# Attention inside a three-part kernel: masks by matmul, value rows in the host's layout, means spread by Pool

## The chip, the cores and the metric

One core of a Trainium2 chip runs one program. The metric is the device time of one execution in microseconds (us); of a kernel the median of its runs is taken.

## The reference

Three parts follow one another. The first is an attention in which each query sees the 31 keys around it and 24 block maxima of the keys; the second a mixture of experts in which each token goes to its best expert; the third a second mixture with a fixed capacity for each expert. The change touches the first alone:

```python
B, H, S, D = q.shape                      # 4, 8, 768, 64
block, window = (32, 16)
k_sum = k.reshape(B, H, nb, block, D).max(axis=3)
v_sum = v.reshape(B, H, nb, block, D).mean(axis=3)
scores_l = scale * np.matmul(q, k.transpose(0, 1, 3, 2))
mask_l = np.abs(pos[:, None] - pos[None, :]) < window
scores_s = scale * np.einsum('bhsd,bhnd->bhsn', q, k_sum) + np.log(block)
scores_l_m = np.where(mask_l, scores_l, -1000000000.0)
scores_all = np.concatenate([scores_l_m, scores_s], axis=-1)
a = np.exp(scores_all - np.max(scores_all, axis=-1, keepdims=True))
a = a / (np.sum(a, axis=-1, keepdims=True) + 1e-09)
return np.matmul(a, np.concatenate([v, v_sum], axis=2))
```

## The kernel before, in words

The attention (function `phase_a`) works on eight units, each a batch element and four of its eight heads. A unit is six steps, so there are 48 steps; a step takes two head pairs by two windows of 64 queries, that is four score tiles of 128 rows (64 queries of each of two heads) by 118 columns: 24 block maxima and 94 keys around the window. Masked columns and the logarithm of the block size come from a table in `cst`, which also holds an identity matrix.

One loop over `i` issues the work of several steps at once, and each engine runs its own part in that order:

- `qk(i)`, L124: four query-key matmuls into a PSUM tile `s_ps` (two buffers). Then VectorE, for each of the four, adds the mask, multiplies by -0.125, writes the result to `s_sb` in SBUF and keeps the minimum in `nm` (one custom instruction and one that reads its accumulator, L132).
- `ptr(i-2)`, L140: four transposes of the weights into `pt_ps` (two buffers), copied to SBUF by ScalarE (L145).
- `ex(i-1)`, L134: four exponentials on ScalarE from `s_sb`, with `nm` as bias (L138). In the loop `ptr` stands ahead of `ex`.
- `pv(i-3)`, L147: sixteen half-width matmuls with the value rows `VV` (three buffers), whose last column of ones gives the sum; VectorE divides (L156 to L164) into `X`.
- In the second unit of each batch element, `post` and `logits` (L165 to L181): transposes of the finished rows, and the router's logits. The routing of the first mixture follows in a few stages on VectorE and Pool, tied to later steps (`gate1` to `gate3`, `first1` to `first3`).
- For the next unit: block maxima (`prep_k`, VectorE), a second set of keys (`prep_k2`, VectorE), the maxima copied into both key tiles (`prep_kc`, L108 and L109, VectorE), the queries spread into a block-diagonal tile (`prep_q`, L112, half by ScalarE and half by VectorE).

`load(u)` issues a unit's transfers on SP's queue, in program order: keys and queries of two head pairs, then the means of the unit before, then values `v` for the means, then the value rows. `prep_v` (L113) makes the means of a unit: Pool adds 32 rows pairwise in SBUF (L118), scales (L120), and four DMAs on SP's queue spread the 24 means of each head to the twelve windows of `VV`:

```python
for h in range(4):
    nc.sync.dma_start(vv[0:24,:,h,0:64],vs2[24*h:24*h+24,None,:].to_broadcast([24,12,64]))
```

What sets the order around the change is thus program order alone, by the loop's lags (`LAGS=(1,2,3)`) and the tables `SHIFT`, `EARLYK` and `STAGES`. A DMA in SP's queue that waits holds up all that stands behind it, and so does a waiting instruction on VectorE, ScalarE or Pool.

Behind the loop come the rest of the routing, the first mixture (`phase_b`) and the second (`phase_d`), which run matmuls with weights split into a high and a low part by ScalarE, VectorE and Pool (L504, L505).

Of the kernel before, what the change touches and what calls it, by code (L numbers as in the profile page):

```python
# [7 lines left out]
AF=mybir.ActivationFunctionType; OP=mybir.AluOpType; AX=mybir.AxisListType  # L8
# [15 lines left out]
def layout(inp):  # L24
    q,k,v=inp['q'],inp['k'],inp['v']
    qd=np.ascontiguousarray(q.reshape(B,4,2,S,D).transpose(0,2,4,1,3)).reshape(B,128,4,S)
    kd=np.zeros((B,2,D,4,KW),np.float32)
# [8 lines left out]

    j=np.arange(94)[None,:]; c=np.arange(128)[:,None]%64
    band=(j>=c)&(j<=c+30)
    m=np.zeros((3,128,118),np.float32)
    m[:,:,:24]=np.float32(8*np.log(32))  # L40
    ok=[band&(j>=15), band, band&(j<=78)]
    for i in range(3): m[i,:,24:]=np.where(ok[i],0.0,NEG)
    cst=np.concatenate([m.transpose(1,0,2).reshape(128,354),np.eye(128,dtype=np.float32)],1).astype(np.float32)
    return dict(q=qd,k=kd,v65=vd,v=np.ascontiguousarray(v),w17=w17,cst=np.ascontiguousarray(cst))

def phase_a(nc,tc,ctx,I,st):
# [27 lines left out]
    def load(u):  # L74
        b,g=units[u]
        kt=ld.tile([128,2,KW],F32,name="kt",bufs=3); qd=ld.tile([128,2,S],F32,name="qd"); vn=st["raw"].tile([128,2048],F32,name="wraw")[0:96]
        vv=VV[u%3]; src=I['v65']
        def ld_k(h0,h1): nc.sync.dma_start(kt[:,h0:h1],I['k'][b,:,2*g+h0:2*g+h1,:])
        def ld_q(h0,h1): nc.sync.dma_start(qd[:,h0:h1],I['q'][b,:,2*g+h0:2*g+h1,:])
        def ld_v():  # L80
            nc.sync.dma_start(vn,I['v'][b,4*g:4*g+4].rearrange("h (n k) d -> (h n) (k d)",k=32))
        def ld_vv():
            for (s0,s1) in ((0,6),(6,12)):
                ap=bass.AP(tensor=src.tensor,offset=src.offset+(b*2+g)*VR*260+64*260*s0,ap=[[260,VP],[64*260,s1-s0],[1,260]])
                nc.sync.dma_start(vv[24:24+VP,s0:s1].rearrange("p s h d -> p s (h d)"),ap)
# [23 lines left out]
        cpy(d['k2'][:,h,:,0:24],ks)  # L109
    def prep_q(u,h,half,cpy):  # L110
        d=U[u]; qd,q2=d['qd'],d['q2']; r=64*half
        cpy(q2[r:r+64,h,:,r:r+64],qd[r:r+64,h].rearrange("p (t c)->p t c",c=64))  # L112
    def prep_v(u,eng):  # L113
        d=U[u]; vn,vv=d['vn'],d['vv']
        vs2=wk.tile([96,64],F32,name="vs2",bufs=2); w=1024
        if eng is V: V.tensor_reduce(vs2,vn[:,w:2*w].rearrange("p (k d)->p d k",d=64),AX.X,OP.add); w//=2
        while w>=64:
            G.tensor_tensor(vn[:,0:w],vn[:,0:w],vn[:,w:2*w],op=OP.add); w//=2  # L118
        if eng is V: G.tensor_tensor(vn[:,0:64],vn[:,0:64],vs2,op=OP.add)
        G.tensor_scalar(vs2,vn[:,0:64],1.0/32,None,op0=OP.mult)  # L120
        for h in range(4):
            nc.sync.dma_start(vv[0:24,:,h,0:64],vs2[24*h:24*h+24,None,:].to_broadcast([24,12,64]))
    X={}; XT={}; D={}
    def qk(i):  # L124
        u,pairs=steps[i]; d=U[u]
        p=ps.tile([128,4,128],F32,name="s_ps")
        for j,(h,w) in enumerate(pairs):
            T.matmul(p[:,j,0:118],d['q2'][:,h,w,:],d['k2'][:,h,w//2,:] if w%2 else d['kt'][:,h,64*w:64*w+118],start=True,stop=True)  # L128
        sb=wk.tile([128,4,118],F32,name="s_sb"); nm=wk.tile([128,4],F32,name="nm")
        for j,(h,w) in enumerate(pairs):  # L130
            mk=mask[:,0 if w==0 else (2 if w==11 else 1),:]
            V.tensor_tensor_reduce(out=sb[:,j,:],in0=p[:,j,0:118],in1=mk,scale=-0.125,scalar=3e38,op0=OP.add,op1=OP.min,accum_out=nm[:,j:j+1])  # L132
        D['sb',i]=(sb,nm)
    def ex(i):  # L134
        sb,nm=D.pop(('sb',i))
        pe=wk.tile([128,4,118],F32,name="p_e")
        for j in range(4):
            A.activation(pe[:,j,:],sb[:,j,:],AF.Exp,bias=nm[:,j:j+1],scale=-1.0)  # L138
        D['pe',i]=pe
    def ptr(i):  # L140
        pt=ps.tile([118,4,128],F32,name="pt_ps")
        pe=D.pop(('pe',i))
        for j in range(4): T.transpose(pt[:,j,:],pe[:,j,:],ident)
        pts=wk.tile([118,4,128],F32,name="pt_sb",bufs=5)
        A.copy(pts,pt)  # L145
        D['pt',i]=pts
# [981 lines left out]
```

## Time and profile before

| what | us |
|---|---|
| median of 3 runs (687.06 to 688.77) | 687.66 |
| the profiled execution | 682.42 |
| its span, first to last instruction | 680.8 |
| PE (TensorE matmuls) busy | 604.4 |
| DVE (VectorE) busy | 508.0 |
| POOL busy | 359.0 |
| ACT (ScalarE) busy | 314.2 |

Busy times are of the whole span and of stages with different limits: the loop of the attention is its first quarter. PE counts matmuls, whose ends are modelled; weight loads stand apart as PEld. The share of the DMA engines can pass 1, since packets overlap. A wait is put down to what came last.

### The profile page before, as it was taken

To read this page: it belongs to the slowest core of one execution; us is meant where nothing else is said; L and a number is where in the kernel's file an instruction comes from. 1 tells how busy PE (TensorE), PEld (TensorE's weight loads), DVE (VectorE), ACT (ScalarE), POOL (GpSimd) and SP (SyncE) were. 2 spreads that over 40 slices of the span, in tenths; PEclk is the share of its full clock that TensorE was granted. 3 is DMA by queue.
4 is the path that set the end of the run, shared out by engine and by line. 5 is a ranking of instruction groups with operands and counts; after the bars stand their busy time and mean duration, and the time that the engine had idled before them with its cause. 6 is when DMAs were issued, how large, how long until landed. Compare 5 with 4: busy or idle time off the path is not lost.

```text
span 680.8 us, 12765 instructions
## 1 busy us (share of the span) xinstructions
PE 604.4 (89%) x4424; PEld 494.0 (73%) x4427; DVE 508.0 (75%) x1896; ACT 314.2 (46%) x672; POOL 359.0 (53%) x388
## 2 busy tenths in 40 slices
PE   8769896899788999989447999999999999999996
PEld 5658775778466776666226778888797978879895
DVE  5788985999896899994675778788888888862120
ACT  6557774787235676461014235162533426154521
POOL 5234323535462463761016359494876939399841
PEclk9889997999689999898559999999999999999999
DMA  9999999969309968610026063453626254385201
GB/s 258 256 241 249 241 234 206 281 115 339 136 16 324 294 207 287 204 62 23 2 87 208 2 227 115 166 175 124 202 76 203 79 187 155 139 258 180 105 1 46
DMA packets 59778, 114.22 MB, mean 168 GB/s; under 512 B 13537, under 2 KB 23521, under 8 KB 58944
## 3 DMA queue, kind: packets, MB, share of 16 engines
q1 hardware_dynamic: 49968, 79.37, 40.6%
q0 software_dynamic: 9744, 34.02, 15.1%
q8 instruction: 35, 0.57, 0.4%
q14 instruction: 31, 0.25, 0.1%
HBM read 96.54 MB, written 14.88 MB: 164 GB/s over the span
## 4 chain that ended last, share of the span: by engine, by line
PE 18%; issue 11%; POOL 11%; DVE 6%; DMA 3%; ACT 1%; POOLq 1%; DVEq 0%
POOL wl L932 9%; PE dh_ps L961 3%; PE dh_ps L962 3%; PE dh_ps L963 3%; DMA xg<-xrows,p_ix 2%; PE dz_ps L975 2%; PE dz_ps L976 2%; PE dz_ps L977 2%; POOL out_dram L982 2%; DMA wraw<-in_w1b_dram 1%; DVE p_g L793 1%; PE rt_ps L806 1%; PE dx_ps L895 1%; PE dh_ps L950 1%; ACT wh L923 1%
## 5 line engine op out<-in xcount | busy, mean ns | idle before, releaser
L932 POOL TENSOR_TENSOR wl<-wraw,wh 128x512 fp32r<-128x512 f32 x124 | 155.4, 1297 | 5.9 <-ACT wh L923 5.5
L961 PE MATMUL dh_ps<-dxh,wh 128*128 128x384 f32 x256 | 89.2, 349 | 0.7 <-ACT dxh L953 0.7
L923 ACT CAST wh<-wraw 128x512 fp32r<-128x512 f32 x128 | 73.7, 620 | 33.8 <-DMA wraw<-in_w1b_dram 33.4
L962 PE MATMUL dh_ps<-dxl,wh 128*128 128x384 f32 x256 | 86.3, 337 | 0.5 <-DVE dxl L953 0.5
L963 PE MATMUL dh_ps<-dxh,wl 128*128 128x384 f32 x256 | 86.1, 336 | 0.0
L118 POOL TENSOR_TENSOR wraw<-wraw 96x512 f32<-96x512 f32 (+4 forms) x39 | 39.9, 1023 | 80.2 <-DMA wraw<-in_v_dram 77.8
L975 PE MATMUL dz_ps<-wh,dhh 128*128 128x512 f32 x192 | 79.0, 411 | 0.0
L977 PE MATMUL dz_ps<-wh,dhl 128*128 128x512 f32 x192 | 76.0, 396 | 0.0
L976 PE MATMUL dz_ps<-wl,dhh 128*128 128x512 f32 x192 | 75.9, 395 | 0.0
L968 DVE SCALAR_TENSOR_TENSOR dhl<-dh_ps,dhh 128x384 fp32r<-128x384 f32 x64 | 35.1, 554 | 49.0 <-ACT dhh L966 48.7
L982 POOL DMA_INDIRECT out_dram<-dz,io x24 | 24.5, 1023 | 79.5 <-ACT dz L980 76.8
L966 ACT ACTIVATE dhh<-dh_ps 128x384 fp32r<-128x384 f32 x64 | 31.5, 492 | 75.7 <-PE dh_ps L963 74.8
L505 POOL TENSOR_TENSOR wl<-wraw,wh 128x512 fp32r<-128x512 f32 (+1 forms) x26 | 47.8, 1861 | 26.2 <-ACT wh L504 22.7
L980 ACT COPY dz<-dz_ps 128x512 f32<-128x512 f32 x24 | 14.1, 587 | 102.8 <-PE dz_ps L977 56.8
L138 ACT ACTIVATE p_e<-s_sb,nm 128x118 f32<-128x118 f32 x192 | 59.7, 385 | 1.1 <-DVE nm L132 1.1
L128 PE MATMUL s_ps<-kt,Q 128*128 128x118 f32 x192 | 41.4, 299 | 11.6 <-DVE kt L108 9.1
L939 POOL DMA_INDIRECT xg<-xrows,p_ix x24 | 23.3, 972 | 50.9 <-DVE rrow L871 31.3
L961 PEld LDWEIGHTS dh_ps<-dxh,wh 128*128 128x128 f32 x256 | 48.4, 189 | 1.5 <-ACT dxh L953 0.9
L962 PEld LDWEIGHTS dh_ps<-dxl,wh 128*128 128x128 f32 x256 | 48.2, 188 | 1.3 <-DVE dxl L953 1.1
L963 PEld LDWEIGHTS dh_ps<-dxh,wl 128*128 128x128 f32 x256 | 48.1, 188 | 0.0
L504 ACT CAST wh<-wraw 128x1024 fp32r<-128x1024 f32 (+1 forms) x48 | 44.2, 983 | 7.3 <-DMA wraw<-in_w1a_dram 7.1
L132 DVE CUSTOM_DVE_ANT_0 s_sb<-s_ps,cst 128x118 f32<-128x118 f32 x192 | 42.0, 275 | 5.3 <-PE s_ps L128 3.5
(359 smaller groups left out, 1466.5 us busy)
## 6 DMA issues: line engine op xcount, KB each, us to landing
wraw<-in_w1b_dram SPq DMA_DIRECT2D x15, 1024.0 KB
wraw<-in_w2b_dram POOLq DMA_DIRECT2D x14, 1024.0 KB, 7.5
wraw<-in_w2a_dram SPq DMA_DIRECT2D x12, 1024.0 KB
wraw<-in_w1a_dram SPq DMA_DIRECT2D x10, 1024.0 KB
VV<-in_v_dram SPq DMA_DIRECT2D x16, 585.0 KB
kt<-in_k_dram SPq DMA_DIRECT2D x16, 412.0 KB
qd<-in_q_dram SPq DMA_DIRECT2D x16, 384.0 KB
wraw<-in_v_dram SPq DMA_DIRECT2D x8, 768.0 KB
```

The source lines that it names most:

```text
L132: V.tensor_tensor_reduce(out=sb[:,j,:],in0=p[:,j,0:118],in1=mk,scale=-0.125,scalar=3e38,op0=OP.add,op1=OP.min,accum_out=nm[:,j:j+1])
L138: A.activation(pe[:,j,:],sb[:,j,:],AF.Exp,bias=nm[:,j:j+1],scale=-1.0)
L504: (hi.tensor_copy if hi else nc.scalar.copy)(h[:,c],t[:,c])
L505: (lo or nc.vector).tensor_tensor(l[:,c],t[:,c],h[:,c].bitcast(F32),op=OP.subtract)
L923: A.copy(h[:,c],t[:,c])
L932: eng.tensor_tensor(l[:,c],t[:,c],h[:,c].bitcast(F32),op=OP.subtract)
L961: T.matmul(q,wh[:,c],s['xh'][:,d,:],start=(d==0),stop=False)
L962: T.matmul(q,wh[:,c],s['xl'][:,d,:],start=False,stop=False)
L963: T.matmul(q,wl[:,c],s['xh'][:,d,:],start=False,stop=(d==3))
L975: T.matmul(q,s['hh'][:,f,c0],wh[:,c],start=(f==0),stop=False)
L976: T.matmul(q,s['hh'][:,f,c0],wl[:,c],start=False,stop=False)
L977: T.matmul(q,s['hl'][:,f,c0],wh[:,c],start=False,stop=(f==7))
```

## The change

The mask is no longer added by VectorE. For each step TensorE first multiplies the identity by two mask tables at a time into `s_ps`, as the start of the sum, and the query-key matmuls add to it. The factor -0.125 moves into `prep_q`, the mask's sign and size change on the host, VectorE takes one minimum over all four tiles, and the exponentials read `s_ps` in PSUM. `s_ps` has three buffers and `pt_ps` one; `ex` stands ahead of `ptr`. The host lays value rows out so that three windows of a partition lie in one piece, and the values for the means are loaded by two DMAs. The means go by four small DMAs to one tile of 24 partitions, and Pool copies them into the twelve windows.

```diff
@@ layout
-NEG=-8e9
+NEG=-1e9
+    vd=vd.reshape(B,2,VR,260)[:,:,np.arange(VP)[:,None]+64*np.arange(12)[None,:]].reshape(B,2,VP,4,780)
+    vd=np.concatenate([vd,np.zeros((B,2,VP,4,4),np.float32)],4)
-    m[:,:,:24]=np.float32(8*np.log(32))
+    m[:,:,:24]=-np.float32(np.log(32))
-    for i in range(3): m[i,:,24:]=np.where(ok[i],0.0,NEG)
+    for i in range(3): m[i,:,24:]=np.where(ok[i],0.0,-NEG)
@@ phase_a
+    def sps(): return ps.tile([128,4,128],F32,name="s_ps",bufs=3)
@@ load
-            nc.sync.dma_start(vn,I['v'][b,4*g:4*g+4].rearrange("h (n k) d -> (h n) (k d)",k=32))
+            vs=I['v'][b,4*g:4*g+4].rearrange("h (n k) d -> (h n) (k d)",k=32)
+            for c in (0,1024): nc.sync.dma_start(vn[:,c:c+1024],vs[:,c:c+1024])
-            for (s0,s1) in ((0,6),(6,12)):
-                ap=bass.AP(tensor=src.tensor,offset=src.offset+(b*2+g)*VR*260+64*260*s0,ap=[[260,VP],[64*260,s1-s0],[1,260]])
-                nc.sync.dma_start(vv[24:24+VP,s0:s1].rearrange("p s h d -> p s (h d)"),ap)
+            for s0 in (0,2): nc.sync.dma_start(vv[24:24+VP,3*s0:3*s0+6].rearrange("p (a s) h d -> p a (s h d)",s=3),src[b,g,:,s0:s0+2,0:780])
@@ prep_q
-        cpy(q2[r:r+64,h,:,r:r+64],qd[r:r+64,h].rearrange("p (t c)->p t c",c=64))
+        o,i=q2[r:r+64,h,:,r:r+64],qd[r:r+64,h].rearrange("p (t c)->p t c",c=64)
+        if cpy is A.copy: A.mul(o,i,-0.125)
+        else: V.tensor_scalar(o,i,-0.125,None,op0=OP.mult)
@@ prep_v
-        for h in range(4):
-            nc.sync.dma_start(vv[0:24,:,h,0:64],vs2[24*h:24*h+24,None,:].to_broadcast([24,12,64]))
+        vs=wk.tile([24,4,64],F32,name="vs",bufs=2)
+        for h in range(4): nc.sync.dma_start(vs[:,h],vs2[24*h:24*h+24])
+        G.tensor_copy(vv[0:24,:,:,0:64],vs[:,None,:,:].to_broadcast([24,12,4,64]))
@@ qk
-        p=ps.tile([128,4,128],F32,name="s_ps")
+        p=sps()
+        mk=[0 if w==0 else (2 if w==11 else 1) for h,w in pairs]
+        for j in (0,2):
+            m=mask[:,mk[j],:]; m=bass.AP(tensor=m.tensor,offset=m.offset,ap=[m.ap[0],[118*(mk[j+1]-mk[j]),2],[1,118]])
+            T.matmul(p[:,j:j+2,0:118],ident,m,start=(j==0),stop=False,skip_group_check=True)
         for j,(h,w) in enumerate(pairs):
-            T.matmul(p[:,j,0:118],d['q2'][:,h,w,:],d['k2'][:,h,w//2,:] if w%2 else d['kt'][:,h,64*w:64*w+118],start=True,stop=True)
+            T.matmul(p[:,j,0:118],d['q2'][:,h,w,:],d['k2'][:,h,w//2,:] if w%2 else d['kt'][:,h,64*w:64*w+118],start=False,stop=(j==3),skip_group_check=True)
-            V.tensor_tensor_reduce(out=sb[:,j,:],in0=p[:,j,0:118],in1=mk,scale=-0.125,scalar=3e38,op0=OP.add,op1=OP.min,accum_out=nm[:,j:j+1])
+        nm=wk.tile([128,4],F32,name="nm")
+        V.tensor_reduce(nm,p[:,:,0:118],AX.X,OP.min)
@@ ex
-            A.activation(pe[:,j,:],sb[:,j,:],AF.Exp,bias=nm[:,j:j+1],scale=-1.0)
+            A.activation(pe[:,j,:],p[:,j,0:118],AF.Exp,bias=nm[:,j:j+1],scale=-1.0)
@@ ptr
-        pt=ps.tile([118,4,128],F32,name="pt_ps")
+        pt=ps.tile([118,4,128],F32,name="pt_ps",bufs=1)
@@ the loop
+        if LE<=i<n+LE: ex(i-LE)
         if LA<=i<n+LA: ptr(i-LA)
-        if LE<=i<n+LE: ex(i-LE)
```

How the order of instructions moves, at three places. On PE, one step of a second unit (`s_ps` scores, `pt_ps` transposed weights, `o_ps` output, `l_ps` logits, `xt_ps` output transposed), before:

```order
L128 MATMUL s_ps<-kt,Q_0_114 128x118
L128 MATMUL s_ps<-K_0_99,Q_0_114 128x118
L128 MATMUL s_ps<-kt,Q_0_114 128x118
L128 MATMUL s_ps<-K_0_99,Q_0_114 128x118
L143 MATMUL pt_ps<-cst,p_e 118x128 x4
L154 MATMUL o_ps<-VV_126,pt_sb 64x65 x8
L178 MATMUL l_ps<-xT,w_98 32x128 x4
L179 MATMUL l_ps<-cst,xT 128x128
L168 MATMUL xt_ps<-cst,X_334 128x128 x4
```

and now:

```order
L138 MATMUL s_ps<-cst 128x2x118 x2
L140 MATMUL s_ps<-kt,Q_0_114 128x118
L140 MATMUL s_ps<-K_0_99,Q_0_114 128x118
L140 MATMUL s_ps<-kt,Q_0_114 128x118
L140 MATMUL s_ps<-K_0_99,Q_0_114 128x118
L153 MATMUL pt_ps<-cst,p_e 118x128 x4
L164 MATMUL o_ps<-VV_126,pt_sb 64x65 x8
L188 MATMUL l_ps<-xT,w_98 32x128 x4
L189 MATMUL l_ps<-cst,xT 128x128
L178 MATMUL xt_ps<-cst,X_326 128x128 x4
```

Two matmuls of two mask tables each (`cst`) stand ahead of the four query-key matmuls; nothing has gone from PE. On VectorE, where the queries of the next unit are spread (`Q` from `qd`, in the middle of a unit), before:

```order
L112 COPY Q_1_119<-qd 64x12x64
L132 ISA s_sb,nm<-s_ps,cst 128x118
L132 ISA nm 128x1
L132 ISA s_sb,nm<-s_ps,cst 128x118
L132 ISA nm 128x1
L132 ISA s_sb,nm<-s_ps,cst 128x118
L132 ISA nm 128x1
L132 ISA s_sb,nm<-s_ps,cst 128x118
L132 ISA nm 128x1
L156 TENSOR_SCALAR rs<-o_ps 128x4
L157 RECIPROCAL rc<-rs 128x4
L162 TENSOR_TENSOR X_922<-o_ps,rc 128x256
```

and now:

```order
L117 TENSOR_SCALAR Q_1_119<-qd 64x12x64
L142 TENSOR_REDUCE nm<-s_ps 128x4
L166 TENSOR_SCALAR rs<-o_ps 128x4
L167 RECIPROCAL rc<-rs 128x4
L172 TENSOR_TENSOR X_1534<-o_ps,rc 128x256
L191 TENSOR_REDUCE lg<-l_ps 128x17
L108 COPY K_1_100<-kt 128x6x94
L117 TENSOR_SCALAR Q_1_119<-qd 64x12x64 x2
```

Eight instructions of the masked minimum have become one reduction, and the query copies are scalings, in some steps two more than before. On ScalarE at the same place, before:

```order
L112 COPY Q_1_119<-qd 64x12x64
L145 COPY pt_sb<-pt_ps 118x512
L138 ACTIVATE p_e<-s_sb,nm 128x118 x4
L180 COPY xT<-l_ps 128x128
L145 COPY pt_sb<-pt_ps 118x512
```

and now:

```order
L148 ACTIVATE p_e<-s_ps,nm 128x118 x4
L155 COPY pt_sb<-pt_ps 118x512
L190 COPY xT<-l_ps 128x128
L180 COPY xT<-xt_ps 128x512
L148 ACTIVATE p_e<-s_ps,nm 128x118 x4
```

No query copy is left on ScalarE, since each `A.copy` makes a new object and `cpy is A.copy` never holds; the exponentials read `s_ps` and stand ahead of the copy of `pt_ps`.

## Rows read from the trace of the kernel before

**Rows 1.** Stretches of the attention loop, busy time of each engine in each:

```profile
core 0: us, PE busy (x) PEld busy (x) DVE busy (x) ACT busy (x) POOL busy (x), PEclk, DMA share, GB/s
6.80:163.30 156.50, 130.02 (x1564) 109.14 (x1565) 128.64 (x682) 106.03 (x292) 56.97 (x85) 0.95 0.97 236
23.20:56.00 32.80, 26.72 (x300) 22.65 (x299) 25.46 (x116) 16.96 (x47) 11.23 (x25) 0.85 1.00 254
56.00:86.70 30.70, 26.50 (x341) 22.12 (x340) 28.54 (x139) 23.17 (x65) 11.64 (x13) 1.00 1.00 245
86.70:130.50 43.80, 34.08 (x424) 28.89 (x423) 33.51 (x179) 28.00 (x77) 15.30 (x19) 0.92 1.05 233
130.50:163.30 32.80, 31.40 (x424) 26.96 (x423) 30.39 (x190) 25.67 (x74) 13.13 (x21) 1.00 0.80 200
```

**Rows 2.** Timeline of PE: the first query-key matmul of six steps (start, us, engine, line):

```profile
6.83 0.34 PE L128 MATMUL s_ps<-kt,Q 128*128 128x118 f32 x1 [0.63 <-DVE Q L112]
...
92.70 0.38 PE L128 MATMUL s_ps<-kt,Q 128*128 128x118 f32 x2
...
95.69 0.38 PE L128 MATMUL s_ps<-kt,Q 128*128 128x118 f32 x2
...
117.27 0.48 PE L128 MATMUL s_ps<-kt,Q 128*128 128x118 f32 x2
...
119.41 0.37 PE L128 MATMUL s_ps<-kt,Q 128*128 128x118 f32 x1
...
160.25 0.38 PE L128 MATMUL s_ps<-kt,Q 128*128 128x118 f32 x2
```

**Rows 3.** What PE waited for in the loop: us in total, times, longest us:

```profile
PE s_ps L128 <- DVE kt L108: 9.1, 2, 6.2
PE o_ps L154 <- issue: 3.7, 1, 3.7
PE xt_ps L168 <- DVE X L162: 3.1, 3, 1.9
PE l_ps L178 <- DVE r_t L355: 2.8, 2, 2.1
PE o_ps L154 <- DMA VV<-vs: 2.1, 5, 0.5
```

**Rows 4.** Prices on PE, from the timeline and the views of lines 638 and 128:

```profile
95.91 0.28 PE L128 MATMUL s_ps<-K,Q 128*128 128x118 f32 x1
...
226.29 0.49 PE L638 MATMUL lgp<-lr,pk 128*128 128x192 f32 x2
...
L638 PE MATMUL lgp<-lr,pk x20: 322/327/686, 226.3 to 324.9; 128*128 128x192 f32 x10, 64*128 64x192 f32 x10
...
L128 PE MATMUL s_ps<-K,Q x192: 275/275/422, 7.1 to 161.0; 128*128 128x118 f32 x192
```

**Rows 5.** Groups by line on DVE and ACT to 290 us (count, busy us, mean ns, idle before):

```profile
L132 DVE CUSTOM_DVE_ANT_0 s_sb<-s_ps,cst 128x118 f32<-128x118 f32 x192 | 42.0, 275 | 5.3 <-PE s_ps L128 3.5 <-PE pt_ps L143 0.9 <-ACT p_e L138 0.4
...
L101 DVE TENSOR_REDUCE ks<-kt 128x24 f32<-128x768 f32 x16 | 15.2, 947 | 11.5 <-DMA kt<-in_k_dram 11.5
L112 DVE COPY Q<-qd 64x768 f32<-64x768 f32 x16 | 14.4, 900 | 0.5
...
L112 ACT COPY Q<-qd 64x768 f32<-64x768 f32 x16 | 13.3, 829 | 1.3 <-DMA qd<-in_q_dram 1.3
...
L108 DVE COPY kt<-ks 128x144 f32<-128x144 f32 x16 | 8.6, 540 | 0.6 <-ACT K L105 0.2
...
L105 DVE COPY K<-kt 128x564 f32<-128x564 f32 x12 | 6.3, 526 | 0.0
...
L181 DVE TENSOR_REDUCE lg<-l_ps 128x17 f32<-128x68 f32 x23 | 5.1, 223 | 3.3 <-ACT xT L180 2.6
```

**Rows 6.** Groups of Pool in the loop:

```profile
L118 POOL TENSOR_TENSOR wraw<-wraw 96x512 f32<-96x512 f32 (+4 forms) x39 | 39.9, 1023 | 80.2 <-DMA wraw<-in_v_dram 77.8
...
L312 POOL CAST it<-cb 128x768 bf16<-128x768 f32 x1 | 0.8, 827 | 0.0
...
L309 POOL CAST it_b<-cb 128x128 bf16<-128x128 f32 x1 | 0.3, 288 | 0.0
```

**Rows 7.** Timelines of Pool's and of SP's queue, first and fifth unit:

```profile
17.34 0.40 POOL L120 TENSOR_SCALAR vs<-wraw 96x64 f32<-96x64 f32 x1
...
1.78 0.43 SPq L89 DMA_DIRECT2D cst<-in_cst_dram  x1
...
72.43 0.54 SPq L81 DMA_DIRECT2D wraw<-in_v_dram  x1
...
85.75 4.40 SPq L122 DMA_DIRECT2D VV<-vs  x4
90.19 0.54 SPq L81 DMA_DIRECT2D wraw<-in_v_dram  x1
```

**Rows 8.** Timeline of 43 to 46 us, and the view of line 108 (ns, smallest/median/largest):

```profile
43.62 2.33 POOL L118 TENSOR_TENSOR wraw<-wraw 96x1024 f32<-96x1024 f32 x1 [12.16 <-DMA wraw<-in_v_dram]
43.68 2.37 DVE L108 COPY kt<-ks 128x144 f32<-128x144 f32 x1
...
46.10 0.37 PE L128 MATMUL s_ps<-kt,Q 128*128 128x118 f32 x1 [2.91 <-DVE kt L108]
...
L108 DVE COPY kt<-ks x16: 225/235/2369, 5.2 to 146.5; 128x144 f32<-128x144 f32 x16
```

**Rows 9.** DMA packets to 165 us:

```profile
DMA packets 29211, 39.20 MB, mean 238 GB/s; under 512 B 11045, under 2 KB 21029, under 8 KB 28420
```

**Rows 10.** Timeline behind the loop:

```profile
168.73 4.30 DVE L504 CAST wh<-wraw 128x512 fp32r<-128x512 f32 x1
...
169.02 1.29 POOL L505 TENSOR_TENSOR wl<-wraw,wh 128x512 fp32r<-128x512 f32 x1
...
173.14 0.31 PE L1100 MATMUL s_ps<-cb,xg 128*128 128x128 f32 x1 [2.08 <-DMA xg<-xrows,r_gx]
```

More of the change, by code (lines that the diff above doesn't have):

```diff
@@ L57, in phase_a @@
     wm=K2[1][:,0].rearrange("p a b->p (a b)")[:,0:256]; V.memset(wm,1.0); wm=wm.bitcast(BF)
+    def sps(): return ps.tile([128,4,128],F32,name="s_ps",bufs=3)
     def spin(k,wm=wm):
-        p=ps.tile([128,4,128],F32,name="s_ps").rearrange("p a b->p (a b)")
+        p=sps().rearrange("p a b->p (a b)")
         for _ in range(k): T.matmul(p,wm[:,0:128] if len(wm.shape)==2 else wm[:,0,0:128],wm,start=True,stop=True)
@@ L125, in qk @@
         u,pairs=steps[i]; d=U[u]
-        p=ps.tile([128,4,128],F32,name="s_ps")
-        for j,(h,w) in enumerate(pairs):
-            T.matmul(p[:,j,0:118],d['q2'][:,h,w,:],d['k2'][:,h,w//2,:] if w%2 else d['kt'][:,h,64*w:64*w+118],start=True,stop=True)
-        sb=wk.tile([128,4,118],F32,name="s_sb"); nm=wk.tile([128,4],F32,name="nm")
-        for j,(h,w) in enumerate(pairs):
-            mk=mask[:,0 if w==0 else (2 if w==11 else 1),:]
-            V.tensor_tensor_reduce(out=sb[:,j,:],in0=p[:,j,0:118],in1=mk,scale=-0.125,scalar=3e38,op0=OP.add,op1=OP.min,accum_out=nm[:,j:j+1])
-        D['sb',i]=(sb,nm)
+        p=sps()
[3 more added lines that the diff above has]
+            T.matmul(p[:,j:j+2,0:118],ident,m,start=(j==0),stop=False,skip_group_check=True)
+        for j,(h,w) in enumerate(pairs):
+            T.matmul(p[:,j,0:118],d['q2'][:,h,w,:],d['k2'][:,h,w//2,:] if w%2 else d['kt'][:,h,64*w:64*w+118],start=False,stop=(j==3),skip_group_check=True)
+        nm=wk.tile([128,4],F32,name="nm")
+        V.tensor_reduce(nm,p[:,:,0:118],AX.X,OP.min)
+        D['sb',i]=(p,nm)
     def ex(i):
-        sb,nm=D.pop(('sb',i))
+        p,nm=D.pop(('sb',i))
         pe=wk.tile([128,4,118],F32,name="p_e")
         for j in range(4):
-            A.activation(pe[:,j,:],sb[:,j,:],AF.Exp,bias=nm[:,j:j+1],scale=-1.0)
+            A.activation(pe[:,j,:],p[:,j,0:118],AF.Exp,bias=nm[:,j:j+1],scale=-1.0)
         D['pe',i]=pe
     def ptr(i):
-        pt=ps.tile([118,4,128],F32,name="pt_ps")
+        pt=ps.tile([118,4,128],F32,name="pt_ps",bufs=1)
         pe=D.pop(('pe',i))
@@ L193, in gate1 @@
             A.activation(d,d,AF.Exp)
-            r=st['route1'].group(c,n,m,lambda:ps.tile([128,4,128],F32,name="s_ps").rearrange("p a c->p (a c)") if b==B-1 else ps.tile([128,512],F32,name="l_ps",bufs=1)); next(r)
+            r=st['route1'].group(c,n,m,lambda:sps().rearrange("p a c->p (a c)") if b==B-1 else ps.tile([128,512],F32,name="l_ps",bufs=1)); next(r)
             D['gd',c]=d,r
@@ L213, in first1 @@
         if t==5:
-            D['first']=st['route1'].first(lambda:ps.tile([128,4,128],F32,name="s_ps").rearrange("p a c->p (a c)")); next(D['first']); st['raw0']()
+            D['first']=st['route1'].first(lambda:sps().rearrange("p a c->p (a c)")); next(D['first']); st['raw0']()
     def first2(b,t):
@@ L266, in phase_a @@
         for s in splits.get(i-n,()): st['split'](*s)
-        if i in (n+1,n+2): st['warm'](ps.tile([128,4,128],F32,name="s_ps").rearrange("p a c->p (a c)"),2)
-        if i==n+2: x0=ps.tile([128,4,128],F32,name="s_ps"); st['xT0'](x0,0)
+        if i in (n+1,n+2): st['warm'](sps().rearrange("p a c->p (a c)"),2)
+        if i==n+2: x0=sps(); st['xT0'](x0,0)
         if i==n+3: st['xT0'](x0,1)
```

## The prediction, made before the change was run

> **What bounds the kernel now.** The change touches only the attention loop, so I read the table of stretches first and ask who is busy there. The loop takes 156.5 us of the span of 680.8. In it TensorE is busy for 130.0 us, VectorE 128.6, ScalarE 106.0, Pool 57.0, and the DMA engines' share is 0.97 [rows 1]. So TensorE, VectorE and the DMA engines all look close to full, and the averages can't say which one sets the pace.
>
> Steps can. Successive steps of a second half-batch (with the output transposes and the router's logits) start 2.99 us apart, and those of a first half 2.14 us apart [rows 2]; within them PE's instructions follow one another without a wait. The other steps differ from these by holes. PE's waits say what ends them: VectorE's copies of the block maxima into the keys (9.1 us in two waits), one wait of 3.7 us ahead of the first value matmuls, and means that were still being spread by DMA (2.1 us) [rows 3]; smaller ones wait for VectorE's part of the routing. In two stretches TensorE's granted clock is 0.85 and 0.92 of full, after such holes [rows 1]; 1.2 GHz is half, so the part of a stretch at the lower level is twice what is missing.
>
> That gives PE's slack. Idle: 156.5 - 130.0 = 26.5 us. Clock: (1 - 0.85) x 2 x 32.8 = 9.8 us and (1 - 0.92) x 2 x 43.8 = 7.0 us at half speed, of which half is lost: 8.4 us. PE's own work in the loop is then 130.0 - 8.4 = 121.6 us, and all that better loads or a shorter VectorE could ever give back is 34.9 us.
>
> **The change, part by part.**
>
> *Masks on PE.* Each of the 48 steps gets two matmuls of the identity against 2 x 118 mask columns. A float32 matmul runs here as two passes: the order has four query-key matmuls a step, the trace 2 x 192 / 48 = eight. So 48 x 2 x 2 = 192 passes of 236 columns. The trace has none that wide with this type. The nearest is 192 columns: two take 0.49 us and one lasts 0.327, so the second starts 0.163 us after the first; for 118 columns it is 0.39 - 0.275 = 0.115 [rows 4]. In proportion to the columns 236 cost 0.163 x 236 / 192 = 0.200 us; on the line through both points 0.192; as two passes of 118, 0.230. I take 0.200, the nearest row scaled: 192 x 0.200 = **+38.4 us of PE work** (36.9 to 44.2). Nothing is removed from PE.
>
> *Minimum on VectorE.* 192 masked minima, 42.0 us busy or 0.875 a step, become 48 reductions of 4 x 118 = 472 elements. A reduction of 68 takes 0.223 and one of 768 takes 0.947 [rows 5]: 1.034 ns an element, 0.64 us. Saved: 48 x 0.235 = 11.3 us.
>
> *Query copies.* The code means to leave half of the scaled copies on ScalarE, but the order shows all 32 on VectorE (the test of the bound method is never true). VectorE gains 16 x 0.558 = 8.9 us, ScalarE loses 16 x 0.829 = 13.3 [rows 5]. VectorE nets 128.6 - 11.3 + 8.9 = 126 us in a loop that PE stretches past 160, ScalarE about 93. Neither ends last in a step, so 0, except at the start: the first steps wait for both halves, now one behind the other, about +0.6 us.
>
> *Score buffers and order.* A score buffer is now held until the exponentials have read it, and there are three; the exponentials stand ahead of the copy of the transposed weights. With one transpose buffer the next transposes wait for that copy, which ScalarE does a step earlier. ScalarE has some 65 us of room in the loop: 0. If ScalarE were late by a step, PE would wait there next.
>
> *Loads.* Value rows go from 9216 packets of 1040 bytes to 3072 of 3120; the spreading of means from 9216 packets of 256 bytes (most of the 11045 under 512 [rows 9]) to 768. SP's four issues for the means took 4.40 us, where a plain one takes 0.43 [rows 7]: about 1.7 instead, so each next load starts some 2.7 us earlier. The DMA share falls well under 1, and holes that wait for keys or means should close. This is a gain on the waits alone, counted below.
>
> *Means on Pool.* Eight copies of 12 x 4 x 64 = 3072 elements. A one-input cast of 768 took 0.827 us [rows 6]; five two-input additions, 1024 + 512 + 256 + 128 + 64 = 1984 elements, took 5.44 [rows 8]: 3.3 to 8.4 us each; I take 3.3, the row with one input. Pool goes from 57 to 83 us. The copy waits for its four small transfers; behind it stand the next unit's additions. It fits: additions 5.4, issues 1.7, a landing and the copy 3.3 against 160 / 8 = 20 us a unit. Only the first unit has no lead: its means were late already (the 3.7 us), and one shorter issue plus a copy of 3.3 in place of a landing leaves PE, itself 5 x 0.8 us later, waiting about 2.5.
>
> **The sum.** PE's work 121.6 + 38.4 = 160.0 us is a floor for the loop, 3.5 over its present length, with no hole left. Holes that I keep: 2.5 for the first means, 1.0 for the clock behind that, 0.6 for the query copies, and 2 for the routing's steps on VectorE and for copies that collide with Pool: 6 us. Loop 166 us, **+9.4 us**. What lies behind the loop starts when it ends, so it moves along at 0. The profiled execution took 682.42 us and becomes 691.8; it lies 5.2 under the median of the runs, 687.66, so the median goes to **697.0 us**.
>
> **Rivals.**
>
> *A. Collisions of VectorE and Pool take the place of the loads (slower still).* For: a copy of 144 columns that takes 0.235 lasted 2.37 us when it began just behind a Pool addition, and PE waited for it [rows 3, 8]. The query copies have a median of 0.558 but a mean of 0.900 [rows 5]: 16 x 0.342 = 5.5 us. The change doubles them and adds half to Pool's time: 5.5 x 2 x 83 / 57 = 16 us, 10.5 more. Against: VectorE has 40 us of room. If all of it reaches PE: 707.5. It decides if a unit's first step waits for VectorE by over 1 us each time. The Trainium skill, "SBUF — State Buffer", section "Who interferes with whom", states that VectorE's copies and tensor-scalar operations in a two-port mode and any Pool instruction exclude each other for a whole instruction, which speaks against spreading by Pool. The 2.37 us agree with it. By that rule each Pool copy may hold VectorE for up to its full length, 8 x 3.3 = 26 us at worst, which is more than this sum has.
>
> *B. Every hole closes.* Loop at its floor, +3.5: 691.2. For: SP and the DMA engines are relieved in every unit. Against: the first unit, and the routing's holes, which no load causes.
>
> *C. The end pays back (faster).* Behind the loop VectorE's pair of casts takes 4.64 us where the pair before it took 0.76, and PE waits 2.08 for gathered rows [rows 10]. If the first expert's weights, which now come up to 4 x 0.8 us earlier against the last step, and the new timing remove both (3.9 + 2.1), and the loop stays at its floor, the sum is 3.5 - 6.0 = -2.5: 685.2. It decides only where the loop loses less than 3.8 us. Against: casts and gather follow the last steps in program order.
>
> *D. The masks cost one pass each.* 19.2 in place of 38.4: 677.8. Against: every float32 matmul with other weights than a transpose has two.
>
> **How the numbers follow.** A measurement of this kernel tells about 0.3% (2.1 us) from no change. Forecast, loop +5 to +14: 0.62. Rival A, or means late in each unit, beyond that: 0.14. Rival B up to the forecast's edge: 0.08. Between -2 and +2, the floor with part of C: 0.09. C: 0.06; D: 0.01. So faster 0.07, same 0.09, slower 0.84. The range: 689 (B with a little of C) to 708 (A in full, or passes at 0.230 us, +5.8, with four more of waits).
>
> **What would show it.** Right: 2 matmuls a step on 236 columns, second pass some 0.20 us after the first; steps some 2.9 and 3.8 us apart; clock near 1 from 30 us on; PE busy over 95% of the loop; DMA share far under 0.97; the loop about 166 us. Wrong: passes well under 0.2; holes that remain at the units' starts with VectorE or Pool as their end; a stretch from the loop's end to the first expert that is shorter by 5 us or more.

## The result, and the profile after

The changed kernel took 695.32 us (median of 4 runs, 692.64 to 696.28), the kernel before, on the same chip, 687.36 us (4 runs, 684.42 to 688.77): ratio 1.0112, 95% interval 1.0072 to 1.0153, slower by 8.0 us. The forecast was 697.0, slower. It was right on the side and nearly on the size, but the nearness is partly luck: TensorE's own work in the loop is 5 us less than I had said, its idle time and its clock cost 10 us more, and the kernel before had been profiled in an execution 5 us under its median.

The profiled execution took 695.01 us with a span of 693.4, against 682.42 and 680.8. Stretches of the attention loop of the changed kernel, with the columns of [rows 1]:

```profile
7.50:178.40 170.90, 158.29 (x1760) 139.88 (x1759) 139.79 (x368) 93.36 (x278) 81.95 (x94) 0.97 0.72 211
7.50:54.20 46.70, 36.69 (x349) 32.75 (x347) 31.77 (x67) 20.38 (x60) 20.19 (x20) 0.89 0.81 217
54.20:95.20 41.00, 40.79 (x470) 35.96 (x470) 37.21 (x100) 24.22 (x74) 21.27 (x30) 1.00 0.82 250
95.20:138.60 43.40, 41.00 (x471) 35.91 (x470) 39.48 (x104) 24.53 (x75) 20.46 (x21) 1.00 0.70 206
138.60:178.40 39.80, 39.80 (x474) 35.26 (x474) 31.32 (x100) 24.24 (x73) 20.03 (x24) 1.00 0.54 171
```

The loop takes 170.9 us, 14.4 more than the 156.5 of [rows 1]; I had said 166. TensorE is busy in 158.3 of it. From 54 us on it has hardly any room left: 40.8 of 41.0, 41.0 of 43.4, 39.8 of 39.8 us, at a clock of 1.00. Most of what goes wrong lies in the first stretch, with 10 us idle and a clock of 0.89. What TensorE waited for in the loop (us in total, times, longest):

```profile
PE o_ps L164 <- POOL VV L128: 10.0, 2, 7.2
PE pt_ps L153 <- ACT pt_sb L155: 1.6, 1, 1.6
PE s_ps L140 <- DVE kt L111: 0.8, 1, 0.8
PE xt_ps L178 <- DVE X L172: 0.2, 1, 0.2
```

The waits of [rows 3] for the key maxima (9.1), the routing (2.8) and `X` (3.1) have shrunk or gone, and the two for Pool's copies of the means are new. Starts of steps, from the timeline of TensorE, two of a first half-batch and two of a second:

```profile
78.79 0.38 PE L140 MATMUL s_ps<-kt,Q 128*128 128x118 f32 x2
...
81.72 0.38 PE L140 MATMUL s_ps<-kt,Q 128*128 128x118 f32 x2
...
95.27 0.38 PE L140 MATMUL s_ps<-kt,Q 128*128 128x118 f32 x2
...
99.06 0.38 PE L140 MATMUL s_ps<-kt,Q 128*128 128x118 f32 x2
```

They are 2.93 and 3.79 us apart, where [rows 2] had 2.14 and 2.99: 0.79 and 0.80 more, for four passes a step, so 0.20 us a pass. The new prices, by line (of line 138, 142 and 117: ns, smallest/median/largest; of line 128 the group, with mean and idle before):

```profile
L138 PE MATMUL s_ps<-cst x192: 360/362/762, 6.6 to 175.1; 128*128 128x236 f32 x192
...
L142 DVE TENSOR_REDUCE nm<-s_ps x48: 630/642/651, 8.6 to 176.5; 128x4 f32<-128x472 f32 x48
...
L117 DVE TENSOR_SCALAR Q<-qd x32: 542/558/3583, 5.7 to 155.9; 64x768 f32<-64x768 f32 x32
...
L128 POOL COPY VV<-vs 24x3072 f32<-24x3072 f32 x8 | 21.9, 2736 | 54.8 <-DMA vs<-vs 50.4 <-PE s_ps L140 4.4
```

How the first two units' means reach TensorE, from the timelines of Pool, SP's queue and TensorE:

```profile
13.90 5.43 POOL L123 TENSOR_TENSOR wraw<-wraw 96x1024 f32<-96x1024 f32 x5 [7.75 <-DMA wraw<-in_v_dram]
19.42 0.40 POOL L125 TENSOR_SCALAR vs<-wraw 96x64 f32<-96x64 f32 x1
24.29 2.74 POOL L128 COPY VV<-vs 24x3072 f32<-24x3072 f32 x1 [4.48 <-DMA vs<-vs]
...
35.96 0.32 POOL L124 TENSOR_TENSOR wraw<-wraw,vs 96x64 f32<-96x64 f32 x1 [5.50 <-DVE vs L121]
...
41.27 2.73 POOL L128 COPY VV<-vs 24x3072 f32<-24x3072 f32 x1 [4.53 <-DMA vs<-vs]
...
19.84 3.21 SPq L127 DMA_DIRECT2D vs<-vs  x4
...
27.08 1.14 PE L164 MATMUL o_ps<-VV,pt_sb 118*64 118x65 f32 x16 [7.23 <-POOL VV L128]
```

The means are summed at 19.82. The four issues take until 23.05, the last transfer lands at 24.29, Pool's copy ends at 27.03, and the value matmuls start at 27.08: 7.3 us from sum to use. The kernel before took 4.5, from 17.74 (the end of the scaling in [rows 7]) to 22.22:

```profile
17.76 3.60 SPq L122 DMA_DIRECT2D VV<-vs  x4
...
22.22 1.01 PE L154 MATMUL o_ps<-VV,pt_sb 118*64 118x65 f32 x16 [3.68 <-issue]
```

In the changed kernel VectorE, whose instructions run in program order, stands behind TensorE's stall, so its share of unit 1's sum starts only at 33.88 (Pool waits 5.50 us for it), and the second copy stalls TensorE again, for 2.7 us.

### The profile page after: what moved, and what is told of

It reads as the page before. It is cut to its first block, busy times and chain, and to the rows that moved or that the text cites. A ratio compares the mean times of both kernels' runs of the same rounds, so it can differ in the third digit from the quotient of the medians.

```text
span 693.4 us, 12803 instructions
## 1 busy us (share of the span) xinstructions
PE 632.5 (91%) x4619; PEld 526.0 (76%) x4619; DVE 517.4 (75%) x1576; ACT 300.3 (43%) x656; POOL 385.4 (56%) x396
## 2 busy tenths in 40 slices
DMA packets 46081, 112.06 MB, mean 162 GB/s; under 512 B 5217, under 2 KB 5985, under 8 KB 46016
## 4 chain that ended last, share of the span: by engine, by line
PE 21%; issue 10%; POOL 9%; DVE 6%; DMA 3%; ACT 1%; POOLq 0%; DVEq 0%
POOL wl L942 7%; PE dh_ps L971 4%; PE dh_ps L972 4%; PE dh_ps L973 4%; PE dz_ps L985 2%; PE dz_ps L986 2%; PE dz_ps L987 2%; DMA xg<-xrows,p_ix 2%; POOL out_dram L992 1%; DVE p_g L803 1%; PE rt_ps L816 1%; DMA wraw<-in_w1b_dram 1%; ACT wh L933 1%; PE dx_ps L905 1%; PE rt_ps L812 0%
## 5 line engine op out<-in xcount | busy, mean ns | idle before, releaser
L942 POOL TENSOR_TENSOR wl<-wraw,wh 128x512 fp32r<-128x512 f32 x124 | 155.5, 1294 | 4.7 <-ACT wh L933 4.4
L148 ACT ACTIVATE p_e<-s_ps,nm 128x118 f32<-128x118 f32 x192 | 53.5, 369 | 13.5 <-DVE nm L142 10.7
L128 POOL COPY VV<-vs 24x3072 f32<-24x3072 f32 x8 | 21.9, 2736 | 54.8 <-DMA vs<-vs 50.4
L138 PE MATMUL s_ps<-cst 128*128 128x236 f32 x192 | 49.9, 383 | 0.4 <-DMA cst<-in_cst_dram 0.4
```

Source lines behind the costliest of these rows:

```text
L138: T.matmul(p[:,j:j+2,0:118],ident,m,start=(j==0),stop=False,skip_group_check=True)
L148: A.activation(pe[:,j,:],p[:,j,0:118],AF.Exp,bias=nm[:,j:j+1],scale=-1.0)
L942: eng.tensor_tensor(l[:,c],t[:,c],h[:,c].bitcast(F32),op=OP.subtract)
```

## The experiments

Loops run from the first query-key product to the end of TensorE's work in the 48th turn of the loop; what lags behind the last steps comes after that. All kernels were timed against the kernel before, in three batches, each on one chip.

**One part at a time.** The value rows in the new layout, and the raw values in two transfers, on the kernel before:

```diff
-            nc.sync.dma_start(vn,I['v'][b,4*g:4*g+4].rearrange("h (n k) d -> (h n) (k d)",k=32))
+            vs=I['v'][b,4*g:4*g+4].rearrange("h (n k) d -> (h n) (k d)",k=32)
+            for c in (0,1024): nc.sync.dma_start(vn[:,c:c+1024],vs[:,c:c+1024])
...
-                nc.sync.dma_start(vv[24:24+VP,s0:s1].rearrange("p s h d -> p s (h d)"),ap)
+            for s0 in (0,2): nc.sync.dma_start(vv[24:24+VP,3*s0:3*s0+6].rearrange("p (a s) h d -> p a (s h d)",s=3),src[b,g,:,s0:s0+2,0:780])
```

with the change's host layout. Expected:

> The kernel before with the loads of the change alone: value rows in one piece of 3120 bytes for three windows, values for the means by two DMAs; masks on VectorE and means spread by four DMAs as before. Theory (PE's own work in the loop is 121.6 us, the holes are mostly late loads): the waits for keys and for spread means go, the routing's holes stay, VectorE with 128.6 us of work becomes the next bound; loop 138 to 148 us in place of 156.5, time 8 to 18 us under before. Rival (the loads were hidden, and VectorE or the routing set the holes): loop within 3 us of 156.5.

Measured: 683.72 us, ratio 0.9907 (0.9880 to 0.9934). The loop is 156.4 us, just as before, although the DMA share fell from 0.97 to 0.90. The longest waits of TensorE in it:

```profile
PE o_ps L156 <- DMA VV<-vs: 5.2, 7, 2.0
PE s_ps L130 <- DVE kt L110: 4.7, 3, 3.4
PE xt_ps L170 <- DVE X L164: 2.9, 2, 2.2
PE l_ps L180 <- DVE r_t L357: 2.6, 1, 2.6
```

So the rival holds, not the theory: with the loads relieved, the same kinds of wait stand at other steps. TensorE was idle for 21.2 us in place of 26.5, but its clock was 0.91 over the loop in place of 0.95 [rows 1], and the one took back what the other gave. The median is lower by 0.9%. Against the control further down, the same kernel as before with a loop of 159.7 us, this loop is 3.3 us shorter and the median 0.1% lower, so what the loads are worth here is open.

The masks on TensorE alone. It is the change with that diff turned round, and with the means spread by DMA as in the kernel before:

```diff
-        G.tensor_copy(vv[0:24,:,:,0:64],vs[:,None,:,:].to_broadcast([24,12,4,64]))
+            nc.sync.dma_start(vv[0:24,:,h,0:64],vs2[24*h:24*h+24,None,:].to_broadcast([24,12,64]))
```

> The change without its loads: masks on PE, three score buffers, query scaling on VectorE, but value rows in pieces of 1040 bytes, one DMA for the values, means spread by four DMAs. Theory (38.4 us of masks fill the holes that late loads left, so the loads matter little once PE is the bound): loop 163 to 172 us, time 6 to 16 us over before. Rival (masks and late loads add up): loop 180 to 195 us, time 25 to 38 us over before.

Measured: 690.05 us, 1.0028 (1.0006 to 1.0050), loop 164.4. As the theory said for the loop; the time is only 0.4 to 3.4 us over before, where I had 6 to 16; I had counted from the first profile's loop, a short one (see the control). The waits in it are 6.8 us in all, of which 3.8 are the first means; those for VectorE are 2.4, without any new load. So the longer work of TensorE closed the holes: the other engines have 0.8 us more in each step. With cheaper masks, further down, they come back.

The change with the new loads as they are, and that last edit alone, so without Pool's copies:

> The change with one part undone: the means go to the twelve windows by four DMAs again, not by Pool. Theory (Pool's wait and copy of 2.7 us make the first unit's means late, the stall of 7.2 us on PE holds up VectorE's half of the second unit's means, and that makes the second stall of 3.0 us): the first stall falls to about 4.5 us, the second goes; loop 164 to 167 us in place of 170.9, time 4 to 7 us under the change. Rival (the stall comes from the values, which land 2 us later as two DMAs, not from Pool): loop within 1.5 us of 170.9.

And with the edit for the first two units only, so that Pool spreads the means of six units out of eight:

```diff
+        if u<2:
+            for h in range(4):
+                nc.sync.dma_start(vv[0:24,:,h,0:64],vs2[24*h:24*h+24,None,:].to_broadcast([24,12,64]))
+        else:
...
```

> The change with the means of units 0 and 1 alone spread by DMA, those of the other six by Pool. Theory (only the first two units have no lead; the six later copies lie beside other work): loop and time within 1 us of the run with all means spread by DMA. Rival (Pool's copies hold up VectorE's two-port copies in every unit): 3 to 8 us slower than that run.

Measured: 688.61 us, 1.0015 (0.9977 to 1.0053), loop 164.0, and 688.25 us, 1.0006 (0.9976 to 1.0037), loop 163.8: both theories hold. The pair settles two things. Against the masks alone (164.4), the new loads are worth next to nothing in a loop that TensorE bounds. And spreading by Pool costs 7 us, for the first two units, where the copy has no lead; six copies with a lead cost nothing here. The values for the first means land between 11.8 and 13.9 us in the profiles, with one transfer as with two, so it isn't the split transfer that makes the stalls. Waits of the kernel with the first two units by DMA:

```profile
PE o_ps L168 <- issue: 3.4, 1, 3.4
PE s_ps L144 <- DVE kt L111: 1.8, 2, 1.2
PE xt_ps L182 <- DVE X L176: 0.6, 1, 0.6
PE o_ps L168 <- DMA VV<-vs: 0.5, 2, 0.4
```

The means cost 3.9 us there in place of 10.0, and the clock over the loop is 0.99 in place of 0.97; the waits for VectorE are 2.4, as with the masks alone, at other steps.

**The query copies.** The change with half of them on ScalarE:

```diff
-        if cpy is A.copy: A.mul(o,i,-0.125)
+        if cpy==A.copy: A.mul(o,i,-0.125)
```

> The change with every second scaled query copy really on ScalarE (16 of 32). Theory (TensorE and the late first means set the loop, VectorE has room): loop within 1.5 us of the change's 170.9, time within 0.3% of the change, so about 1.008 to 1.014 of the kernel before; the first query-key matmul comes about 0.6 us earlier. Rival (the query copies on VectorE, which collide with Pool's work, feed the holes): VectorE's query copies drop from 32.1 to about 16 us, the holes of 7.6 and 3.0 us shrink, and the loop falls by 3 us or more.

And beside it the change itself again:

> The change itself on the same chip as the three runs beside it: 1.007 to 1.015 of the kernel before, loop 169 to 172 us with TensorE stalled 10 us at the value matmuls of the first two units, if those stalls are the change's own; if they were chance of one execution, loop 164 to 167.

Measured: 691.45 us, 1.0092 (1.0059 to 1.0125), loop 166.9; the change again 697.81 us, 1.0167 (1.0096 to 1.0238), loop 171.0, with the same two stalls (7.2 and 2.7 us). The stalls are the change's own. The query copies were worth 4.0 us of loop, so the rival holds, not my theory that VectorE has room: the two stalls at the means are 8.9 us in place of 10.0, and the other waits (2.6 us) are gone. One place where they cost is the start of the sixth unit. In the change, from the timelines of Pool, VectorE and TensorE:

```profile
114.79 2.74 POOL L128 COPY VV<-vs 24x3072 f32<-24x3072 f32 x1 [4.43 <-PE s_ps L140]
...
103.17 3.58 DVE L117 TENSOR_SCALAR Q<-qd 64x768 f32<-64x768 f32 x1
...
114.98 2.69 DVE L111 COPY kt<-ks 128x144 f32<-128x144 f32 x1
...
117.73 0.48 PE L140 MATMUL s_ps<-kt,Q 128*128 128x118 f32 x2 [0.79 <-DVE kt L111]
```

and with half of the copies on ScalarE:

```profile
113.78 2.80 POOL L128 COPY VV<-vs 24x3072 f32<-24x3072 f32 x1 [4.43 <-PE s_ps L140]
...
113.33 0.22 DVE L111 COPY kt<-ks 128x144 f32<-128x144 f32 x1
...
113.90 0.64 DVE L142 TENSOR_REDUCE nm<-s_ps 128x4 f32<-128x472 f32 x1
```

A copy of 0.23 us lasts 2.69 when it starts 0.2 us into Pool's copy of the means, and ends just after it; here it comes late because a query copy before it, beside Pool's routing work and additions, had lasted 3.58 in place of 0.56, and VectorE had no wait in between in which to catch up. In the other kernel it is done when Pool starts, takes 0.22, and the reduction that then lies beside Pool takes its usual 0.64. The rule in the Trainium skill, "SBUF — State Buffer", section "Who interferes with whom", agrees: such copies of VectorE and Pool exclude each other for a whole instruction. Whether a collision is paid depends on what falls into those 2.7 us.

The change without Pool's copies and with half of the query copies on ScalarE:

> The change with the means spread by DMA and half of the query copies on ScalarE; masks in float32 as in the change. Theory (TensorE's work of 160 us is then the whole loop but for the first hole of 3 to 4 us and its clock): loop 162 to 164, time 0.995 to 1.002 of the kernel before. Rival (query copies on VectorE cost about 4 us wherever they are): loop 159 to 161.

Measured: 686.74 us, 1.0011 (0.9983 to 1.0039), loop 160.9 against 164.0: the rival again. Part of the 3.1 us is only shifted, since the first product started at 8.75 instead of 7.24 us; by the first expert's first matmul (185.44 against 187.23) 1.8 us are left. By the profiles VectorE's query copies thus cost about 2 us without Pool's copies and 4 beside them; the first of these the times don't show (1.0011 against 1.0015, with intervals of 0.3% to either side).

**Cheaper masks.** Masks and identity in bfloat16, one pass instead of two. The block means' factor of 1/32 moves into the value table, so that the masks hold only zeros and one large number whose rounding in bfloat16 doesn't matter:

```diff
-    m[:,:,:24]=-np.float32(np.log(32))
+    m[:,:,:24]=0.0
...
-        G.memset(t[0:24,:,:,64:65],1.0); VV.append(t)
+        G.memset(t[0:24,:,:,64:65],32.0); VV.append(t)
...
-        G.tensor_scalar(vs2,vn[:,0:64],1.0/32,None,op0=OP.mult)
+        G.tensor_scalar(vs2,vn[:,0:64],1.0,None,op0=OP.mult)
...
-            T.matmul(p[:,j:j+2,0:118],ident,m,start=(j==0),stop=False,skip_group_check=True)
+            T.matmul(p[:,j:j+2,0:118],identb,m,start=(j==0),stop=False,skip_group_check=True)
```

> The change with masks and identity in bfloat16, one pass each, the factor 1/32 of the block means folded into the value table (block sums beside 32 in the ones column) so that the masks are exact; means by Pool as in the change. Theory (TensorE's mask passes are the price): 96 passes of about 0.10 us in place of 192 of 0.20 take 29 us off TensorE's work, its floor in the loop falls from 160 to about 131, and with the first units' holes of 10 us and some new ones where VectorE (about 126 us) and the routing end last, the loop is 142 to 152 us and the time 665 to 678. Rival (as the run of the loads alone suggests, VectorE and the routing set a pace near 156 whatever TensorE does): loop 154 to 162, holes spread over the units' starts, time 678 to 688.

The same, with the first two units' means by DMA and half of the query copies on ScalarE:

> The same with the means of the first two units spread by DMA and half of the query copies on ScalarE. Theory: the first holes of 10 us shrink to about 4, VectorE falls to about 117 us; loop 134 to 145, time 655 to 670, faster than the kernel before and the change. Rival (pace of VectorE and routing): loop 150 or more, time 675 or more, and hardly different from the run with Pool alone.

And with all means by DMA:

> Masks in bfloat16 (one pass), value rows in the new layout, half of the query copies on ScalarE, and the means of every unit spread by DMA: no copies on Pool. Theory (copies on Pool and VectorE that fall on each other make the holes that came back with the cheap masks): without the eight Pool copies, six of which ran in the run before, Pool falls from 75 to about 57 us, the holes past the first two units lose at least half of their 13 us, loop 145 to 150, time 676 to 682. Rival (the holes come from VectorE's own work in the routing and at the units' starts, whoever spreads the means): loop 152 to 156, time within 0.3% of that run's 685.

Measured: 693.08 us, 1.0094 (1.0056 to 1.0131); 685.24 us, 0.9985 (0.9956 to 1.0014); 682.56 us, 0.9928 (0.9895 to 0.9961). Their loops, with the columns of [rows 1], in this order:

```profile
7.50:176.10 168.60, 136.44 (x1664) 117.71 (x1665) 142.95 (x368) 92.24 (x278) 82.53 (x94) 0.92 0.71 208
```

```profile
7.94:161.45 153.51, 134.85 (x1666) 116.77 (x1665) 125.05 (x350) 102.09 (x293) 74.71 (x91) 0.96 0.80 229
```

```profile
7.29:164.35 157.06, 136.47 (x1664) 117.17 (x1663) 116.26 (x349) 102.11 (x293) 56.63 (x85) 0.95 0.89 237
```

The pass has the price I gave it: steps of 3.20 us, two passes for 0.21 over the kernel before. But 29 us less work on TensorE shortened the loop by 2.3 us (170.9 to 168.6): VectorE, with collisions, was busy for 143 us, and TensorE fell back into waiting for it. Spreading the first means by DMA and taking half of the query copies off VectorE gave 15.1 us, and with all means by DMA 11.5. The theory on the price held, its sum did not; the rival, that something near 156 us sets the pace whatever TensorE does, fits the second and third (153.5 and 157.1); the first lies above even that, with 13.0 us of waits for the first two units' means. Without Pool's copies, VectorE fell from 125 to 116 us busy and the loop didn't get shorter (157.1), which speaks against collisions as the main cause of those holes. That profile was of its slowest run (685.71 us), so by its median a shorter loop is likelier; this is not settled. What TensorE waited for there, longest first:

```profile
PE o_ps L164 <- DMA VV<-vs: 6.0, 4, 5.2
PE s_ps L140 <- DVE kt L112: 5.0, 4, 3.8
PE l_ps L188 <- DVE lg L191: 3.8, 2, 2.8
```

**A control.** The kernel before, measured as one of the kernels:

> The kernel before as one of the kernels measured, for a second profile of it. Ratio 0.997 to 1.003. If the holes of its loop are fixed by its order, loop 156 to 157 us with the two waits of about 6 and 3 us for the key maxima again; if they come from how loads and Pool happen to fall against VectorE, other steps hold them and the loop lies anywhere from 154 to 162, which would place the gain of the run with the loads alone in such holes.

Measured: 684.69 us, 0.9970 (0.9938 to 1.0003), loop 159.7. Its waits, to be held against [rows 3]:

```profile
PE s_ps L128 <- DVE kt L108: 4.3, 1, 4.3
PE l_ps L178 <- DVE lg L181: 4.0, 1, 4.0
PE o_ps L154 <- issue: 3.8, 1, 3.8
PE xt_ps L168 <- DVE X L162: 3.7, 2, 3.1
PE o_ps L154 <- DMA VV<-vs: 3.3, 5, 1.8
```

The same program has other holes and a loop 3.2 us longer, so they are not fixed by the order. The first profile, on which the prediction rests, caught the shorter of the two loops. Two kernels came out faster than both the one before, by intervals that leave out 1, and the changed one: the new loads alone (683.72) and cheap masks without Pool (682.56). By medians they gain 0.1 and 0.3% on this control (684.69), and 0.9 and 0.7% on the runs of before beside them; how much of the gain is real is open.

## Why the prediction was right, and where it was wrong

**Right: the price of the masks.** 192 passes at 0.200 us: the steps became 0.79 to 0.80 us longer, four times 0.20. The masks alone gave a loop of 164.4 us, and past the first units every kernel with float32 masks is held by TensorE but for 0 to 3 us. The reduction at 0.64 us measured 0.642. Rival D falls: a float32 pass pair stayed a pair.

**Wrong: TensorE's own work.** I put the floor at 160.0 us. Measured: 158.3 busy less 3.3 for the clock, 155.0 us; from the run without Pool's copies (157.1 busy, clock 0.99) about 155.5. The clock's 3.3 is less than half of the roughly 10 us at the lower level, because TensorE stood still in a part of them, as these stretches of the changed kernel show (columns of [rows 1]):

```profile
24.00:26.00 2.00, 0.00 (x0) 0.00 (x0) 1.99 (x2) 0.00 (x0) 1.71 (x1) 0.50 0.78 227
28.00:30.00 2.00, 2.00 (x10) 1.66 (x8) 0.83 (x4) 0.00 (x0) 1.84 (x3) 0.50 1.03 267
```

By stretches of 2 us, the busy time lost to the clock is 0.5, 1.0 and 0.2 from 26 to 32 us and 1.0 and 0.7 from 44 to 48. So the 121.6 us read for the kernel before were 4.5 to 5 too many, although the steps without a wait grew by the full 0.80. In steps with a wait, part of the waiting counts as busy; one such place, two steps of the kernel before:

```profile
68.86 0.60 PE L143 MATMUL pt_ps<-cst,p_e 128*118 128x128 f32 x4
...
71.67 1.17 PE L143 MATMUL pt_ps<-cst,p_e 128*118 128x128 f32 x4 [0.51 <-ACT p_e L138]
```

The four transposes take 0.60 us with their weights ready and 1.17 when they follow ScalarE's exponentials, all of it busy, at a clock of 1.00. That such places make up the whole 5 us is not shown. The 8.4 us that I took off for the clock before has a slip as well: from 105 to 110 us the clock was 0.85 with TensorE idle all the while, and by the same count the busy time lost was 7.0, so the reading should have been about 123.

**Wrong: the holes that I kept.** The first means were to cost 2.5 us; they cost 10.0 in two stalls, and 3.3 us of clock in place of 1.0. The steps that failed are two. One is SP's four issues, "about 1.7 instead" of 4.40: 96 packets in place of 1152 were issued in 3.21 us, against 3.60 in the first unit before, hardly faster, and the 4.40 of [rows 7] was the slowest of eight, the others 3.30 to 3.60. The copy took 2.74, where I had 3.3, but stands behind the landing rather than in its place, so the path from sum to use became 2.8 us longer. The other is "PE, itself 5 x 0.8 us later": it came to the first value matmuls at 19.85 us, before at 18.54, 1.3 later, for the masks filled holes of its first steps (from 10 to 14 us it had been busy for 2.99 of 4.00). The means were summed 2.1 us later as well (19.82 against 17.74), which no term held and no run explains. Together 3.7 + 2.8 + 2.1 - 1.3 = 7.3, the first stall. What I had not written down is the second unit: VectorE waits for TensorE, and its half of the next sum with it. The loop then is 155.0 + 12.6 idle + 3.3 = 170.9, where I had 160.0 + 5 + 1 = 166. Of my own signs, TensorE busy for over 95% of the loop (93%) and a clock near 1 from 30 us on (0.50 again from 44 to 46) did not come.

**Wrong: "Loads ... a gain on the waits".** Loads alone gave a loop of 156.4, no shorter than the first profile's and 3.3 shorter than the control's, and took next to nothing off the masks' loop (164.4 to 164.0). With the masks on TensorE the holes closed without the new loads. The packets did fall, from 59778 to 46081 in the whole program.

**Wrong in size: the query copies**, 0.6 us forecast, and that at the start alone; 2 to 4 measured by the profiles, with the 4 beside Pool's copies.

**Rival A** named the right mechanism at the wrong scale: collisions reached TensorE with 2.4 us (the waits for `kt` and `pt_sb`), or 4.0 by the run that took half of the query copies off VectorE, not 10.5; its sign, a wait of over 1 us for VectorE at each unit's first step, did not come (one wait there, of 0.8). **Rival B** is excluded by the 10.0 us. **Rival C** came true in part. I had what lies behind the loop move along at 0; the gather wait of 2.08 us [rows 10] is gone, and the casts are quick:

```profile
181.07 0.79 DVE L514 CAST wh<-wraw 128x512 fp32r<-128x512 f32 x2
...
185.45 0.60 PE L1110 MATMUL s_ps<-cb,xg 128*128 128x128 f32 x4
...
194.22 0.77 PE L582 MATMUL h_ps<-wh,xh 128*128 128x512 f32 x1 [0.55 <-DVE r_t L365]
```

The first expert starts 15.9 us after the loop, before 17.3 (180.51 - 163.25): 1.4 us back, in all runs with float32 masks on TensorE. From there to the end it is 499.2 us after 500.3, within the 497 to 502 us that this unchanged part takes in the profiles here.

So of the 14.4 us of loop, some 7.5 are the masks (38.3 us of work, of which the holes absorbed about 31) and 7 the means of the first two units by Pool; the query copies on VectorE make 2 to 4 of these, shared between the two. That is against the first profile's loop. Against the control's (159.7) the masks cost 4.3 and the means still 7; and by the medians the masks with the new loads cost about 1 us (688.25 and 688.61 against 687.42), not clear of the noise. Nearly all of the 8.0 us that were measured is thus the spreading by Pool, with the query copies beside it, and not the masks. The end gave 1.4 back, and the profile of before was 5 us under its median, the profile of the change at its own (695.01 and 695.32). I had added these 5 us to the changed kernel too. That is why 170.9 in place of 166 still ended near the forecast, and that is luck.

## What to carry to other kernels

Where the busiest engine has holes, work added to it is paid only past the holes, and work taken off it returns little, since the waits for the other engines come back: 38 us of added passes cost 4 to 8 us of loop and about 1 us of the median, and taking 29 of them off again gave 2.3 until the first means and VectorE were relieved too. Before counting on a hole, find out whether it is the same in a second execution. A path that gets one more hop (a transfer, then a copy) must be followed for the unit that has no lead, and through the engines that stand in order behind the one that waits.

## What the runs showed that I had not expected

- Four issues on SP's queue between two places of on-chip memory took 3.05 to 3.84 us with 24 packets each, and 3.30 to 5.19 with 288, over all units and profiles: 0.8 us an issue at the least with either, where a plain load's issue takes 0.43 [rows 7].
- The same kernel's loop took 156.5 and 159.7 us, with the long waits at other steps.
- TensorE's clock after a hole: from 24 to 26 us, in the stall of 7.23 us, the granted clock was 0.50 (the 1.2 GHz level) with TensorE idle, and behind the stall four mask passes took 1.94 us in place of 0.96. The first stretch had 0.89, the rest, with hardly a hole, 1.00.
- A Pool copy of 24 x 3072 elements takes 2.74 us, 0.89 ns for each element of a partition, each of the eight times in the changed kernel (2734 to 2739 ns), also beside VectorE, whose instruction paid in the collision shown; the longest of these Pool copies in any run took 2.85.
